# Scores on half the array's rows, the intra product with v streaming, and a DMA transpose for the output

## The chip, the cores and the metric

One core of a Trainium2 chip. It has a matrix engine (TensorE, in the profile PE, its weight loads PEld), three engines that work on vectors (VectorE or DVE, ScalarE or ACT, GpSimd or POOL), a queue processor (SP) and 16 DMA engines. The time is that of one execution on the device in microseconds (us); of several runs the median is given.

## The reference

Two stages. The first is a linear attention with decay, over 4 batches, 8 heads, 768 positions and head size 64; the second an MLP with the Mish function over the 3072 rows that the first gives.

```python
for b in range(nb):                       # blocks along the sequence
    intra = (q_b k_b^T) * Dmask           # lam[h]**(i-j) for i >= j, else 0
    intra = intra @ v_b
    inter = (q_b * lam_pow) @ kv_state
    out[b] = intra + inter
    kv_state = lam_block * kv_state + (k_b * rev_pow)^T @ v_b
x = out as rows of 8 heads x 64           # 3072 x 512
h = x @ w_in                              # 512 -> 2048
out = (h * tanh(softplus(h))) @ w_out     # 2048 -> 512, float32
```

The block size does not matter to the result; the kernel uses blocks of 128 positions.

## The kernel before

The sequence is cut into six **groups** (`NG`) of 128 positions; a group has four **chunks**, one a batch, each of 128 positions and 8 heads. For a group, the MLP works on 4 x 128 = 512 rows: 16 units `mm1_unit` (line 420 for the matmuls, Mish on ScalarE at line 434, result `hsg`) and 16 units `mm2_unit` (line 443; every fourth one ends in a copy by ScalarE and a store to `out`). Every unit is four matmuls with 512 columns.

The order of the program is written out by hand. The loop over groups `n` issues the 32 units of the MLP of group n, and between them the attention **pieces** of group n+1: `room` says after which unit how many pieces follow. Each engine works through its own instructions in that order. In the first place stands `turn` after unit 0, for the first two chunks of the next group.

Group 0 is done ahead in a form of its own (`first_t`, `first_s`, `first_o`): there the scores `pS` of a chunk are computed from `kT[rs]` and `qT[rs]` on 64 rows a head (line 230), the two heads of a pair on the upper and the lower half of the rows, into two tiles. Group 1 turns q and k with TensorE. Groups 2 to 5 are the ones that the change touches. Their q (`qn`) and scaled k (`ktil`, k times a power of lam from `scale_k`, line 259, on POOL except in the last group) are turned by a DMA transpose on SP's queue (`turn`, line 268) into `qraw` and `kraw`, two heads to 128 rows. A chunk is done in two **halves** of four heads, each with three pieces:

- `att_a`: two matmuls `pv` for the state (line 283), into a spare of the MLP's PSUM tiles; VectorE multiplies `qraw` by q's decay `lq` into `qT` (line 318) and copies `kraw` into `kz` (line 322), where each head has its 64 rows and zeros in the other 64; `att_w` brings the state `wst` forward (`raw` on VectorE at 298, `w` on POOL at 299); then `turn` for the chunk after next, or the loads for the next group.
- `att_s`: four score matmuls over all 128 rows (line 358), weights `kz`, moving `qT`; VectorE masks them into `sb` (line 362).
- `att_o`: for each pair of heads one matmul with weights `wst` and moving `qT` (375), and two with weights from `vz` (v with zeros beside it) and moving `sb`, 128 columns (379), so the output comes out turned, features by positions; ScalarE copies it to `xt` (382), the moving operand of `mm1_unit`.

PSUM has eight banks: two each for `ph` and `po` of the MLP, and `pO`, `pS`, `pk`, `pq`, of which the halves of groups 2 to 5 take `pS`/`pk` and `pO`/`pq` in turn. Loads of q, k and v are issued by POOL (lines 69, 77, 80), the stores of `out` by ScalarE.

Of the kernel before, what the change touches and what calls it, by code (L numbers as in the profile page):

```python
# [13 lines left out]
def bc(ap, axis, n):  # L14
    shape = list(ap.shape)
    shape.insert(axis, n)
    return ap.unsqueeze(axis).broadcast_to(shape)
# [3 lines left out]
def kernel(  # L21
# [10 lines left out]
    nc = tc.nc  # L32
# [75 lines left out]
    def load_chunk(i):  # L108
        load_k(i)
        load_q(i)  # L110
        load_v(i)
# [8 lines left out]
    k0 = const.tile([128, H, D], F16, name="k0")  # L120
    q0 = const.tile([128, H, D], F16, name="q0")
    ek = const.tile([128, 1], F32, name="ek")

    load_k(0)
    load_q(0)
# [12 lines left out]
    for s in range(WS):  # L138
        load_wout(s)
    nc.gpsimd.iota(ei, pattern=[[1, C]], base=-MID, channel_multiplier=0,  # L140
                   allow_small_or_imprecise_dtypes=True)
    for i in range(B, 2 * B):
        load_chunk(i)
# [30 lines left out]
    lnp = const.tile([128, JP], F32, name="lnp")  # L174
    lq = const.tile([128, JP, C], F32, name="lq")
    lbc = const.tile([128, JP], F32, name="lbc")

    def decays(t):
        for j in range(JP):
# [11 lines left out]
    def q_decays():  # L191
        nc.vector.tensor_tensor(out=lq, in0=bc(ei, 1, JP), in1=bc(lnp, 2, C), op=ALU.mult)
        nc.scalar.activation(lq, lq, AF.Exp)
        nc.scalar.preload_act_table(AF.Mish)


# [79 lines left out]
    def att_kv(s, spare):  # L276

        n, b, hf = s.n, s.b, s.hf
        i = n * B + b
        pv = ps.tile([128, 2, 128], F32, name="pv", tag=spare, bufs=2)  # L280
        for p in range(2):
            j = 2 * hf + p
            nc.tensor.matmul(  # L283
                pv[:, p, :].rearrange("p (a e) -> p a e", a=2),
                ktil[i][:, 4 * hf + 2 * p : 4 * hf + 2 * p + 2, :].rearrange("p h c -> p (h c)"),
                vz[i % NVB][:, 2 * j : 2 * j + 2, 0:D], start=True, stop=True,
            )
        s.pv = pv
# [17 lines left out]
    def att_a(s):  # L306

        n, b, hf = s.n, s.b, s.hf
        i = n * B + b
        lqh = lq[:, 2 * hf : 2 * hf + 2, :]  # L310
        s.qT = work.tile([128, 2, C], F16, name="qT", tag="qT", bufs=5)
        s.kz = kz[s.seq % NKB]
        kp = [ktil[i][:, 4 * hf + 2 * p : 4 * hf + 2 * p + 2, :].rearrange("p h c -> p (h c)")
              for p in range(2)]
        if n >= NT:
            if n < NG - 1:
                att_kv(s, s.spare)
            nc.vector.tensor_tensor(  # L318
                out=s.qT, in0=qraw[i][:, 2 * hf : 2 * hf + 2, :], in1=lqh, op=ALU.mult)
            for hp in range(2):  # L320
                rs = slice(64 * hp, 64 * hp + 64)
                nc.vector.tensor_copy(s.kz[rs, :, hp, :], kraw[i][rs, 2 * hf : 2 * hf + 2, :])  # L322
            if n < NG - 1:
                att_w(s)
            if hf == 0 and i + 2 < s.loaded:
                turn(i + 2)
            if hf == 1 and i + B < NG * B:
                load_chunk(i + B)
            return
        pk = ps.tile([128, 2, C], F32, name="pk", tag="pk")  # L330
        pq = ps.tile([128, 2, C], F16, name="pq", tag="pq")
        for p in range(2):
            nc.tensor.matmul(pk[:, p, :], kp[p], ident, start=True, stop=True)  # L333
        for p in range(2):
            j = 2 * hf + p
            nc.tensor.matmul(  # L336
                pq[:, p, :], qn[i][:, 2 * j : 2 * j + 2, :].rearrange("p h c -> p (h c)"),
                ident, is_transpose=True, start=(p == 0), stop=(p == 1),
            )
        att_kv(s, s.spare)  # L340
        nc.vector.tensor_tensor(out=s.qT, in0=pq, in1=lqh, op=ALU.mult)
        for hp in range(2):
            rs = slice(64 * hp, 64 * hp + 64)
            nc.scalar.activation(s.kz[rs, :, hp, :], pk[rs], AF.Copy)  # L344
        if hf == 0 and i + 1 < s.loaded:
            scale_k(i + 1)
        elif hf == 0:
            turn(i + 1)
        att_w(s)
        if hf == 1:  # L350
            ahead.pop(0)()

    def att_s(s):

        psS = ps.tile([128, 4, C], F32, name="pS", tag=("pS", "pk")[s.seq % 2 if s.n >= NT else 0])
        for p in range(2):
            for hp in range(2):
                nc.tensor.matmul(  # L358
                    psS[:, 2 * p + hp, :], s.kz[:, p, hp, :], s.qT[:, p, :], start=True, stop=True,
                )  # L360
        s.sb = work.tile([128, 4, C], F16, name="sb", tag="sb", bufs=4)
        nc.vector.tensor_tensor(  # L362
            out=s.sb, in0=psS, in1=bc(maskT, 1, 4), op=ALU.mult)

    def att_o(s):

        n, b, hf = s.n, s.b, s.hf
        i = n * B + b
        if xt[n] is None:
            xt[n] = work.tile([128, JP, GT], F16, name="xt", tag="xt", bufs=2)  # L370
        psO = ps.tile([128, 2, C], F32, name="pO", tag=("pO", "pq")[s.seq % 2 if s.n >= NT else 0])
        vf = vz[i % NVB].rearrange("p h c -> p (h c)")
        for p in range(2):
            j = 2 * hf + p
            nc.tensor.matmul(psO[:, p, :], wst[b][hf][n % 2][:, p, :], s.qT[:, p, :],  # L375
                             start=True, stop=False)
            for hp in range(2):
                o = 4 * D * j + D * hp
                nc.tensor.matmul(psO[:, p, :], vf[:, o : o + 128], s.sb[:, 2 * p + hp, :],  # L379
                                 start=False, stop=(hp == 1))  # L380
        dst = xt[n][:, 2 * hf : 2 * hf + 2, b * C : (b + 1) * C]
        nc.scalar.activation(dst, psO, AF.Copy)  # L382

    seq = [0]

# [127 lines left out]
    for n in range(NG):  # L513
        units = [(mm1_unit, (n, ni)) for ni in range(NKI)]

        two = 2 if n == 0 else 1
        units += [(mm2_unit, (n, b2 + b, part)) for b2 in range(0, B, two) for part in range(WS)
                  for b in range(two)]
        pieces = []
        if n + 1 < NG:  # L520
            pieces = att_pieces(n + 1)
        if n == 0:

            i = max(i for i, (f2, _) in enumerate(pieces) if f2 is att_a)
            pieces[i : i + 3] = pieces[i + 1 : i + 3] + pieces[i : i + 1]

        if n == 0:
            room = dict(zip(range(24, 32), (1, 2, 3, 3, 3, 3, 3, 3)))
        else:
            first = 9 if n == 1 else 6  # L530
            span = len(units) - 4 - first
            room = {first + u: (u + 1) * len(pieces) // span - u * len(pieces) // span
                    for u in range(span)}
        if n == 1:

            for ni in range(3):
                mm1_part(n, ni, 0, GT - C)
                while late and ni < 2:
                    f2, s = late.pop(0)
                    f2(s)  # L540
                    if f2 is att_o:
                        break
        for u, (fn, args) in enumerate(units):
            rest = fn(*args)
            if n > 0 and rest:
                rest()
            if n == 0 and 2 <= u < 2 + nh:
                att_kv(first_halves[u - 2], "po")
                att_w(first_halves[u - 2])
            if n == 0 and u % 2 == 1 and 0 < (u + 1) // 2 < B:  # L550
                scale_k((u + 1) // 2)
            if n == 0 and nh + 2 <= u < nh + 2 + NVB - B:
                nc.vector.memset(vz[u - nh - 2 + B][:, :, D : 2 * D], 0.0)
            if n == 0 and nh + 2 <= u < nh + 2 + NKB:
                nc.vector.memset(kz[u - nh - 2], 0.0)
            if n == 0 and u == 17:
                q_decays()
            if n == 0 and u == 16:
                nc.vector.tensor_scalar(out=maskT, in0=rel, scalar1=0.0, scalar2=None, op0=ALU.is_ge)
            if n == 0 and u == 18:  # L560
                scale_k(B)
            if n > 0 and pieces and u == 0:
                if n > 1:
                    turn((n + 1) * B)
                turn((n + 1) * B + 1)
            for _ in range(room.get(u, 0)):
                f2, s = pieces.pop(0)
                s.spare = "po" if u < NKI - 1 else "ph"
                f2(s)
            if n == 0 and rest:  # L570
                rest()
        if n == 0:
            late = pieces
            while ahead:
                ahead.pop(0)()
# [30 lines left out]
```

## Time and profile before

| | us |
|---|---|
| median of 3 runs (219.08 to 219.74) | 219.31 |
| span of the profiled execution | 218.5 |
| what the median has beside that span | 0.8 |
| TensorE busy in the span | 210.8 (96%) |
| VectorE, ScalarE, POOL busy | 107.5, 104.0, 109.7 |
| first matmul of the MLP of groups 1, 2, 3, 4, 5 | 57.1, 89.2, 122.2, 155.2, 187.3 |

The profile is of one execution; its page gives the span from the first to the last instruction, and no other time of that execution. A line of a group of instructions gives the source line, the engine, the operation, the tiles (written <- read), the shapes and the count; after the bar busy time and the mean duration of one in ns, and after the second bar the engine's idle time ahead of these instructions and what ended it. The duration of a matmul contains the way through the array: consecutive ones overlap, and what one costs is the distance to the start of the next. A line of the chain gives a start, a length, and what ran.

### The profile page before, as it was taken

Reading aid. Unit: us, or ns where it says so; the run is one execution under the profiler, and the core shown is the slowest. Engines: PE = TensorE matmul, PEld = TensorE weight load, DVE = VectorE, ACT = ScalarE, POOL = GpSimd, SP = SyncE. Lnnn points to the kernel's source line nnn. Section 1 sums busy time; section 2 is a strip of 40 time slices with the busy share of each in tenths; the row PEclk is TensorE's granted clock in tenths of the full one; section 3 lists DMA queues with packets and bytes.
Section 4 is the critical chain, followed back from the end, with each engine's and each line's share of the span. In section 5 each row is a group of like instructions: output and inputs, shape, how many; then the busy total and the mean of one; then the engine's idle time right before and its main releaser. Section 6 shows DMA issues by size and latency. Waiting matters only on the chain.

```text
span 218.5 us, 3720 instructions
## 1 busy us (share of the span) xinstructions
PE 210.8 (96%) x1432; PEld 114.4 (52%) x1432; DVE 107.5 (49%) x238; ACT 104.0 (48%) x195; POOL 109.7 (50%) x134
## 2 busy tenths in 40 slices
PE   7799999999999999999999999999999999999993
PEld 2466544577545565455555445556445555444452
DVE  6757661187309995059974049975316532000000
ACT  5355668466665322466332465333466332566120
POOL 7995334889988888239879039775000000000000
PEclk9999999999999999999999999999999999999999
DMA  9999999998999999919999909999921012100112
GB/s 132 146 154 187 205 206 175 156 159 70 179 139 134 120 154 139 205 24 107 105 149 133 182 5 101 116 136 127 195 52 24 0 51 96 48 0 3 48 56 90
DMA packets 101187, 24.62 MB, mean 113 GB/s; under 512 B 93874, under 2 KB 98226, under 8 KB 101170
## 3 DMA queue, kind: packets, MB, share of 16 engines
q0 software_dynamic: 78080, 13.37, 80.7%
q1 hardware_dynamic: 18592, 4.53, 13.7%
q10 hardware_dynamic: 4498, 6.49, 8.7%
q8 instruction: 11, 0.18, 0.3%
q14 instruction: 6, 0.05, 0.1%
HBM read 27.26 MB, written 6.29 MB: 154 GB/s over the span
## 4 chain that ended last, share of the span: by engine, by line
PE 91%; DVE 2%; DMA 2%; ACT 2%; issue 1%; ACTq 0%; DVEq 0%
PE po L443 38%; PE ph L420 37%; PE pS L358 4%; PE pO L379 4%; PE pO L375 2%; PE pv L283 2%; DMA qn<-in_q_dram 2%; PE pO L244 1%; PE busy L162 1%; PE pS L230 1%; DVE sb L234 1%; DVE dm L180 0%; PE pk L333 0%; PE pq L336 0%; DVE pqT L220 0%
## 5 line engine op out<-in xcount | busy, mean ns | idle before, releaser
L443 PE MATMUL po<-wout,hsg 128*128 128x512 f16 (+2 forms) x400 | 92.0, 371 | 0.0
L420 PE MATMUL ph<-xt,win 128*128 128x512 f16 (+2 forms) x404 | 89.8, 369 | 0.4 <-ACT hsg L434 0.2
L434 ACT ACTIVATE hsg<-ph 128x512 f16<-128x512 f32 x96 | 57.0, 597 | 29.9 <-PE ph L420 29.4
L420 PEld LDWEIGHTS <-win 128*128 128x128 f16 x404 | 37.0, 98 | 35.4 <-issue 0.6
L443 PEld LDWEIGHTS <-hsg 128*128 128x128 f16 x400 | 36.2, 98 | 31.7
L299 POOL TENSOR_TENSOR w<-raw,lbm 128x256 f16<-128x256 f32 x32 | 24.3, 760 | 27.6 <-DVE raw L298 27.5
L362 DVE TENSOR_TENSOR sb<-pS,maskT 128x512 f16<-128x512 f32 x40 | 27.4, 684 | 21.4 <-PE pS L358 21.4
L322 DVE COPY kz<-kraw 64x256 f16<-64x256 f16 x64 | 28.9, 452 | 16.3 <-DMA kraw<-ktil 15.3
L455 ACT ACTIVATE osb<-po 128x512 f32<-128x512 f32 (+1 forms) x24 | 14.2, 592 | 41.3 <-PE po L443 41.3
L382 ACT ACTIVATE xt<-pO 128x256 f16<-128x256 f32 x40 | 14.9, 382 | 24.6 <-PE pO L379 22.8
L69 POOL DMA_DIRECT2D kn<-in_k_dram x23 | 21.5, 936 | 4.2 <-DMA win<-in_moe_w_in_dram 1.7
L77 POOL DMA_DIRECT2D qn<-in_q_dram x23 | 20.6, 897 | 5.6 <-DMA wout<-in_moe_w_out_dram 3.3
L80 POOL DMA_DIRECT2D vz<-in_v_dram x24 | 21.7, 904 | 3.3 <-DMA wout<-in_moe_w_out_dram 1.7
L298 DVE TENSOR_TENSOR raw<-pv,w 128x256 f32<-128x256 f32 x32 | 13.5, 422 | 15.9 <-PE pv L283 15.3
L379 PE MATMUL pO<-sb,vz 128*128 128x128 f16 x160 | 17.3, 219 | 0.0
L318 DVE TENSOR_TENSOR qT<-qraw,lq 128x256 f16<-128x256 f16 x32 | 16.8, 524 | 0.0
L259 POOL TENSOR_TENSOR ktil<-kn,lk 128x512 f16<-128x512 f16 x15 | 16.1, 1081 | 0.1
L358 PEld LDWEIGHTS <-kz 128*128 128x128 f16 x160 | 11.9, 98 | 7.9 <-ACT kz L344 0.3
L450 DVE COPY osb<-po 128x128 f32<-128x128 f32 x1 | 0.3, 291 | 32.0 <-PE po L443 32.0
L358 PE MATMUL pS<-qT,kz 128*128 128x128 f16 x160 | 15.6, 219 | 0.1
L375 PE MATMUL pO<-qT,w 128*128 128x128 f16 x80 | 15.3, 219 | 0.1
L379 PEld LDWEIGHTS <-vz 128*128 128x128 f16 x160 | 12.3, 98 | 3.1 <-issue 0.3
(66 smaller groups left out, 118.0 us busy)
## 6 DMA issues: line engine op xcount, KB each, us to landing
out_dram<-osb ACTq DMA_DIRECT2D x23, 256.0 KB, 2.9
vz<-in_v_dram POOLq DMA_DIRECT2D x24, 128.0 KB, 4.9
kn<-in_k_dram POOLq DMA_DIRECT2D x23, 128.0 KB, 4.4
qn<-in_q_dram POOLq DMA_DIRECT2D x23, 128.0 KB, 4.6
wout<-in_moe_w_out_dram POOLq DMA_DIRECT2D x4, 512.0 KB, 16.6
win<-in_moe_w_in_dram POOLq DMA_DIRECT2D x3, 512.0 KB, 10.2
kn<-in_k_dram SPq DMA_DIRECT2D x1, 256.0 KB, 3.1
qn<-in_q_dram ACTq DMA_DIRECT2D x1, 256.0 KB, 3.8
```

Of the source, the lines that this page charges most:

```text
L69: nc.gpsimd.dma_start(out=kn[i], in_=chunk_rows(k, i))
L77: nc.gpsimd.dma_start(out=qn[i], in_=chunk_rows(q, i))
L80: nc.gpsimd.dma_start(out=vz[i % NVB][:, :, 0:D], in_=chunk_rows(v, i))
L299: nc.gpsimd.tensor_tensor(out=w_new, in0=raw, in1=lb, op=ALU.mult)
L322: nc.vector.tensor_copy(s.kz[rs, :, hp, :], kraw[i][rs, 2 * hf : 2 * hf + 2, :])
L358: nc.tensor.matmul(psS[:, 2 * p + hp, :], s.kz[:, p, hp, :], s.qT[:, p, :], start=True, stop=True,)
L362: nc.vector.tensor_tensor(out=s.sb, in0=psS, in1=bc(maskT, 1, 4), op=ALU.mult)
L375: nc.tensor.matmul(psO[:, p, :], wst[b][hf][n % 2][:, p, :], s.qT[:, p, :], start=True, stop=False)
L379: nc.tensor.matmul(psO[:, p, :], vf[:, o : o + 128], s.sb[:, 2 * p + hp, :], start=False, stop=(hp == 1))
L420: nc.tensor.matmul(ph_t[ni][:, lo:hi], win0[min(ni, 2)][:, kc, max(ni - 2, 0) * 128 : max(ni - 2, 0) * 128 + 128] if ni < w else win[ni // ...
L434: nc.scalar.activation(hsg[n][:, ni, :], ph_t.pop(ni), AF.Mish)
L443: nc.tensor.matmul(po[:, lo:hi], hsg[n][:, ki, b * C : (b + 1) * C], wout[part][:, kk, lo:hi], start=(ki == 0), stop=(ki == NKI - 1),)
```

## The change

It is for groups 2 to 5 (`n >= NT`) and leaves groups 0 and 1 as they are. A chunk is no longer cut into halves. Its three pieces are:

- `chunk_a`: four `pv` matmuls into one tile on bank `pq`, the state brought forward in two parts as before, then `turn` for the chunk after next of the group and the loads for the next group. There are no `qT` and no `kz`.
- `chunk_s`: eight score matmuls on 64 rows each, directly from `kraw` and `qraw`, the heads of a pair on different halves of the rows and in different banks (`pS`, `pk`); two masks into `sb`.
- `chunk_o`: the output comes out with positions as rows. For each pair of heads one matmul with weights `qraw` and 128 moving columns of the state, and two with weights `sb` and the 64 columns of a head's v moving. VectorE multiplies the result, while it copies it out of `pO`, by q's decay `lqt` (a number for each position and head) into `xtok`, and a DMA transpose on SP's queue turns it into `xt`.

`lqt` is made once, by a small `iota` on POOL and an exponential on ScalarE. The pieces of a group, twelve in place of 24, stand after units 6 to 23 (9 to 23 for group 2), where the 24 stood after units 6 to 27 (9 to 27).

```diff
+    nc.gpsimd.iota(eq, pattern=[[0, 1]], base=-MID, channel_multiplier=1, ...)
...
+        nc.scalar.activation(lqt, lnb, AF.Exp, scale=eq)
...
-        if n >= NT:
-            if n < NG - 1:
-                att_kv(s, s.spare)
-            nc.vector.tensor_tensor(
-                out=s.qT, in0=qraw[i][:, 2 * hf : 2 * hf + 2, :], in1=lqh, op=ALU.mult)
-            for hp in range(2):
-                rs = slice(64 * hp, 64 * hp + 64)
-                nc.vector.tensor_copy(s.kz[rs, :, hp, :], kraw[i][rs, 2 * hf : 2 * hf + 2, :])
-            if n < NG - 1:
-                att_w(s)
-            if hf == 0 and i + 2 < s.loaded:
-                turn(i + 2)
-            if hf == 1 and i + B < NG * B:
-                load_chunk(i + B)
-            return
...
+    def chunk_a(s):
...
+        if n < NG - 1:
+            pv = ps.tile([128, JP, 128], F32, name="pv", tag="pq")
+            for j in range(JP):
+                nc.tensor.matmul(
+                    pv[:, j, :].rearrange("p (a e) -> p a e", a=2),
+                    ktil[i][:, 2 * j : 2 * j + 2, :].rearrange("p h c -> p (h c)"),
+                    vz[i % NVB][:, 2 * j : 2 * j + 2, 0:D], start=True, stop=True,
+                )
+            for hf in range(2):
+                raw = work.tile([128, 2, 128], F32, name="raw", tag="raw", bufs=3)
+                hs = slice(2 * hf, 2 * hf + 2)
+                nc.vector.tensor_tensor(
+                    out=raw, in0=pv[:, hs, :], in1=wst[b][hf][n % 2], op=ALU.add)
+                nc.gpsimd.tensor_tensor(
+                    out=wst[b][hf][(n + 1) % 2], in0=raw, in1=lbm[:, hs, :], op=ALU.mult)
+        if i + 2 < (n + 1) * B:
+            turn(i + 2)
+        if i + B < NG * B:
+            load_chunk(i + B)
+
+    def chunk_s(s):
...
+        pS = [ps.tile([128, JP, C], F32, name="pS", tag=("pS", "pk")[t]) for t in range(2)]
+        for j in range(JP):
+            for t in range(2):
+                rs = slice(64 * t, 64 * t + 64)
+                nc.tensor.matmul(pS[t][:, j, :], kraw[i][rs, j, :], qraw[i][rs, j, :],
+                                 start=True, stop=True)
+        s.sb = []
+        for t in range(2):
+            s.sb.append(work.tile([128, JP, C], F16, name="sb", tag="sb", bufs=4))
+            nc.vector.tensor_tensor(out=s.sb[t], in0=pS[t], in1=bc(maskT, 1, JP), op=ALU.mult)
+
+    def chunk_o(s):
...
+        psO = ps.tile([128, H, D], F32, name="pO", tag="pO")
+        for j in range(JP):
+            nc.tensor.matmul(
+                psO[:, 2 * j : 2 * j + 2, :].rearrange("p h e -> p (h e)"), qraw[i][:, j, :],
+                wst[b][j // 2][n % 2][:, j % 2, :], start=True, stop=False)
+            for t in range(2):
+                nc.tensor.matmul(psO[:, 2 * j + t, :], s.sb[t][:, j, :],
+                                 vz[i % NVB][:, 2 * j + t, 0:D], start=False, stop=(t == 1))
+        xtok = work.tile([128, H, D], F16, name="xtok", tag="xtok", bufs=2)
+        nc.vector.tensor_tensor(out=xtok, in0=psO, in1=bc(lqt, 2, D), op=ALU.mult)
+        nc.sync.dma_start_transpose(
+            out=xt[n][:, :, b * C : (b + 1) * C], in_=xtok.rearrange("p h e -> p (h e)"))
+
+    def chunk_pieces(n):
...
+        for t in range(B + 1):
+            if t < B:
+                out_ += [(chunk_a, chunks[t]), (chunk_s, chunks[t])]
+            if t >= 1:
+                out_.append((chunk_o, chunks[t - 1]))
+        return out_
...
-            pieces = att_pieces(n + 1)
+            pieces = att_pieces(n + 1) if n + 1 < NT else chunk_pieces(n + 1)
...
-            first = 9 if n == 1 else 6
-            span = len(units) - 4 - first
+            first = 8 if n == 1 else 5
+            span = len(units) - 8 - first
```

More of the change, by code (lines that the diff above doesn't have):

```diff
@@ L122 @@
     ek = const.tile([128, 1], F32, name="ek")
+    eq = const.tile([128, 1], F32, name="eq")
     load_k(0)
@@ L140 @@
     nc.gpsimd.iota(ei, pattern=[[1, C]], base=-MID, channel_multiplier=0,
+                   allow_small_or_imprecise_dtypes=True)
+    nc.gpsimd.iota(eq, pattern=[[0, 1]], base=-MID, channel_multiplier=1,
                    allow_small_or_imprecise_dtypes=True)
@@ L176 @@
     lbc = const.tile([128, JP], F32, name="lbc")
+    lqt = const.tile([128, H], F32, name="lqt")
     def decays(t):
@@ L353, in att_s @@
     def att_s(s):
-        psS = ps.tile([128, 4, C], F32, name="pS", tag=("pS", "pk")[s.seq % 2 if s.n >= NT else 0])
+        psS = ps.tile([128, 4, C], F32, name="pS", tag="pS")
         for p in range(2):
@@ L370, in att_o @@
             xt[n] = work.tile([128, JP, GT], F16, name="xt", tag="xt", bufs=2)
-        psO = ps.tile([128, 2, C], F32, name="pO", tag=("pO", "pq")[s.seq % 2 if s.n >= NT else 0])
+        psO = ps.tile([128, 2, C], F32, name="pO", tag="pO")
         vf = vz[i % NVB].rearrange("p h c -> p (h c)")
@@ L382, in att_o @@
         nc.scalar.activation(dst, psO, AF.Copy)
+    class Chunk:
+        pass
+    def chunk_a(s):
+        n, b = s.n, s.b
+        i = n * B + b
+        if n < NG - 1:
[17 more added lines that the diff above has]
+            load_chunk(i + B)
@@ new lines, in chunk_s @@
+    def chunk_s(s):
+        i = s.n * B + s.b
+        pS = [ps.tile([128, JP, C], F32, name="pS", tag=("pS", "pk")[t]) for t in range(2)]
[8 more added lines that the diff above has]
+            nc.vector.tensor_tensor(out=s.sb[t], in0=pS[t], in1=bc(maskT, 1, JP), op=ALU.mult)
@@ new lines, in chunk_o @@
+    def chunk_o(s):
+        n, b = s.n, s.b
+        i = n * B + b
+        if xt[n] is None:
+            xt[n] = work.tile([128, JP, GT], F16, name="xt", tag="xt", bufs=2)
+        psO = ps.tile([128, H, D], F32, name="pO", tag="pO")
[10 more added lines that the diff above has]
+            out=xt[n][:, :, b * C : (b + 1) * C], in_=xtok.rearrange("p h e -> p (h e)"))
@@ L384 @@
+    def chunk_pieces(n):
+        chunks = []
+        for b in range(B):
+            s = Chunk()
+            s.n, s.b = n, b
+            chunks.append(s)
+        out_ = []
+        for t in range(B + 1):
[4 more added lines that the diff above has]
+        return out_
     seq = [0]
```

## The prediction

> **What bounds the kernel now.** I read the first two parts of the page, then the waits, the chain that ended last, and TensorE in windows cut at the group borders which that chain shows.
>
> ```profile
> span 218.5 us, 3720 instructions
> PE 210.8 (96%) x1432; PEld 114.4 (52%) x1432; DVE 107.5 (49%) x238; ACT 104.0 (48%) x195; POOL 109.7 (50%) x134
> PEclk9999999999999999999999999999999999999999
> ...
> PE ph L420 <- ACT hsg L434: 0.2, 1, 0.2
> ```
>
> TensorE is busy for 96% of the span, and it never waits long for a result: the one wait of its matmuls inside the groups is 0.2 us. The chain names the borders and the windows add up what lies between them (columns: length, then busy time and instructions of each engine, then granted clock).
>
> ```profile
> 89.19 6.04 PE ph L420 x28
> 97.18 0.22 PE pS L358 x4
> 118.72 3.45 PE po L443 x16
> 122.18 6.04 PE ph L420 x28
> ...
> 57.08:89.19 32.11, 31.87 (x229) 17.81 (x228) 20.05 (x40) 14.36 (x28) 28.46 (x33) 1.00 1.76 141
> 89.19:122.18 32.99, 32.99 (x226) 17.89 (x224) 20.64 (x40) 14.68 (x28) 21.08 (x24) 1.00 1.19 119
> 122.18:155.16 32.98, 32.98 (x225) 17.89 (x224) 20.92 (x42) 14.68 (x28) 18.82 (x22) 1.00 1.04 115
> 155.16:187.26 32.10, 32.10 (x210) 16.99 (x208) 12.05 (x33) 14.68 (x28) 0.00 (x0) 1.00 0.21 56
> ```
>
> Those four windows are the four passes of the group loop that carry attention groups 2 to 5, the work that is changed. TensorE fills the last three to the hundredth. A pass has 128 matmuls of 512 columns at 6.04/28 = 0.2157 us, 27.61 us; in the second window the other 5.38 us are 96 attention matmuls of 128 columns, 0.056 each. The last window has 16 `pv` matmuls fewer and is 0.89 shorter: 0.0556 each, which I use. So in these passes time is the number of columns streamed, and whatever leaves TensorE's stream leaves the span, as long as no wait appears.
>
> **TensorE, part by part.** Per chunk (four a pass, 16 in all) the kernel now has 4 `pv`, 8 score and 4 + 8 output matmuls, 24 x 0.0556 = 1.33 us. `pv` stays at four.
>
> *The intra product.* Eight matmuls of 128 columns become eight of 64. No matmul of 64 columns is in the trace. The two known sizes give (215.7 - 55.6)/384 = 0.417 ns a column and 2.2 ns fixed: 28.9 ns for 64. The ends are 26.7 (nothing fixed) and 55.6 (the weights, which still have 128 columns, or the issue set the pace). Two rows speak for the low end, a weight load and the densest burst:
>
> ```profile
> 15.07 0.11 PEld L244 LDWEIGHTS <-vz 128*128 128x128 f16 x2
> 14.74 0.40 PE L230 MATMUL pS<-pqT,pkT 64*128 64x128 f16 x8 [0.30 <-DVE pqT L220]
> 15.07 0.34 PE L244 MATMUL pO<-sb,vz 128*128 128x128 f16 x3
> 16.84 0.39 PE L244 MATMUL pO<-sb,vz 128*128 128x128 f16 x4
> 17.07 0.38 PE L162 MATMUL busy<-kzero 128*128 128x512 f16 x1
> 17.38 0.40 PE L230 MATMUL pS<-pqT,pkT 64*128 64x128 f16 x8
> 17.92 0.32 PE L420 MATMUL ph<-xt,win 128*128 128x384 f16 x1
> ...
> L230 PE MATMUL pS<-pqT,pkT 64*128 64x128 f16 x32 | 2.0, 260 | 1.4 <-ACT pkT L218 0.8 <-DVE pqT L220 0.6
> L358 PEld LDWEIGHTS <-kz 128*128 128x128 f16 x160 | 11.9, 98 | 7.9 <-ACT kz L344 0.3 <-issue 0.2
> ```
>
> Two full weight loads of 98 ns fit in 0.11 us, so a second can start some 10 to 15 ns after the first; and eight 64-row matmuls with eight loads of their own start within 0.40 - 0.22 = 0.18 us, 26 ns apiece. Neither loads nor issue need 55 ns. I take 28.9: 8 x (55.6 - 28.9) = 0.214 us a chunk, 3.42 us in all.
>
> *The scores.* They become eight matmuls on 64 rows in two halves of the array, exactly the form of L230 in group 0, so the price is in the trace. The pairs run side by side, but not for free at the edges. After the 512-column matmul at 17.07 the next should start at 17.07 + 0.216 = 17.29; the 64-row burst starts at 17.38, 0.094 late. The burst at 14.74 is followed by a full-height matmul at 15.07, 0.33 after its first start, where four pairs at 0.0556 are 0.22. So a burst occupies 0.094 + 0.33 = 0.424 us against 8 x 0.0556 = 0.445: 0.02 gained a chunk, 0.33 us in all. The ends: 0.22 without any edge (3.5 us gained), and one more edge of 0.1 (1.3 us lost). The value taken is the row's own, of the same shape behind the same neighbour.
>
> [...]
>
> Sum on TensorE: 1.33 becomes 0.222 + 0.424 + 0.222 + 8 x 0.0289 = 1.10; 16 x 0.235 = 3.75 us less.
>
> **The other engines.**
>
> ```profile
> L322 DVE COPY kz<-kraw 64x256 f16<-64x256 f16 x64 | 28.9, 452 | 16.3 <-DMA kraw<-ktil 15.3
> L362 DVE TENSOR_TENSOR sb<-pS,maskT 128x512 f16<-128x512 f32 x40 | 27.4, 684 | 21.4 <-PE pS L358 21.4
> L318 DVE TENSOR_TENSOR qT<-qraw,lq 128x256 f16<-128x256 f16 x32 | 16.8, 524 | 0.0
> L298 DVE TENSOR_TENSOR raw<-pv,w 128x256 f32<-128x256 f32 x32 | 13.5, 422 | 15.9 <-PE pv L283 15.3
> L299 POOL TENSOR_TENSOR w<-raw,lbm 128x256 f16<-128x256 f32 x32 | 24.3, 760 | 27.6 <-DVE raw L298 27.5
> L382 ACT ACTIVATE xt<-pO 128x256 f16<-128x256 f32 x40 | 14.9, 382 | 24.6 <-PE pO L379 22.8
> L268 SPq DMA_TRANSPOSE qraw<-qn x16: 1188/1212/2046, 51.7 to 158.6; - x16
> DMA to landing us min/median/max: 2.4/3.7/6.3
> ...
> 9.85 0.28 ACT lk L488
> POOL qn L77 <- DMA wout<-in_moe_w_out_dram: 3.3, 2, 1.7
> ```
>
> VectorE loses the `kz` copies and the `qT` products (45.7 us) and gains 16 `xtok` products of the size of `sb`, 0.68 us each; ScalarE loses 32 `xt` copies of 0.38. None of it was on the path, so it is worth nothing by itself; what covers it is the other engines' idle half. The new `iota` stands on POOL in a stretch where POOL waits for weights anyway (3.3 us, last row), the new exponential is one of the size of `lk`, 0.28 us of ScalarE beside the second matmul of group 0: nothing. POOL's `w` products, scalings and loads keep their number, but come in bunches of four a pass, sooner.
>
> *The new waits.* (a) `pO` has one buffer, and the last two output pieces stand one unit apart. The second needs the first's `xtok`: 0.17 us until the last matmul has drained, 0.68, two hand-overs of 0.03: 0.91 us, against a unit of 0.86 and the 0.03 of the last matmul. About 0.06 a pass, 0.25 in all (0 to 0.5). (b) TensorE now reads `kraw` itself, where VectorE used to be late for it without harm (15.3 us of waits in four places). In the later passes eleven units of 0.86 us lie between the piece that turns the last chunk and its scores, and POOL has some 5.5 us to do in between (three loads, two `w`, a scaling), so some 5 us are left for a landing. In the pass from 57.08 it is close: two transposes there start at 64.86 and 73.18, and land 3 to 5 us later:
>
> ```profile
> 64.86 1.19 SPq L268 DMA_TRANSPOSE kraw<-ktil  x1
> 73.18 1.19 SPq L268 DMA_TRANSPOSE kraw<-ktil  x1
> 72.08 1.07 POOL L259 TENSOR_TENSOR ktil<-kn,lk 128x512 f16<-128x512 f16 x1
> ...
> 64.84 0.11 PE pv L283 x2
> ...
> L69 POOL DMA_DIRECT2D kn<-in_k_dram x23 | 21.5, 936 | 4.2 <-DMA win<-in_moe_w_in_dram 1.7
> ```
>
> The first piece stays at 64.84; twelve units of 0.863 and 3.1 us of attention later, at 78.3, the chunk turned by the second is scored, and its transpose lands at 76 to 79: 0.3 us taken, 0 to 1.5. (c) The output goes through SP. Sixteen more transposes of 1.2 us bring SP to 12 a pass, 14 of 32 us. SP takes them in order, behind `kraw` of the last chunk, which waits for POOL; that one is long gone by then. Behind the last `xtok` stand the turns of the next group, needed some 8 us into the next pass. What counts is the last transpose: the next group's first matmul needs all four chunks. Its cover is eight units of the second matmul, 32 x 0.2157 = 6.90 us. Its chain is 0.2 + 0.68, up to 0.7 behind its predecessor on SP, and the landing: 4.6 to 5.3 us at the median of 3.7, 7.2 to 7.9 at the longest. I take 0.25 us over three passes; the fourth has no loads beside it. Ends: 0 and 3.
>
> Sum: -3.75 + 0.25 + 0.3 + 0.25 = -2.95 us. The profiled span goes from 218.5 to 215.6; the median of the runs, 219.31, has 0.8 around that span, and goes to 216.4.
>
> **The rivals.**
> 1. *The output's transpose lands late (slower).* Loads run beside it, and the passes show DMA shares above 1. If each of the first three passes has a landing of 7.5 us instead of 4, TensorE idles 1.5 to 2 us at each border: 3 x 1.8 - 3.2 gives 221.5. It turns the sign from about 7 us a landing on. Against it: no landing of a transpose in the trace is over 6.3.
> 2. *The 64-column matmuls cost 55.6 ns.* Only the 0.33 of the scores is left, less 0.7 of waits: 219.7, no change. The weight-load and burst rows speak against it. [...]
> [...]
> 4. *`kraw` is late for the scores* in the pass from 57.08 and now and then after: 2 us more, 218.4.
>
> **How the numbers follow.** The forecast has 0.58, rival 1 0.15, rival 2 0.11, rival 3 0.05, rival 4 0.11. This kernel's runs tell a change from none from about 0.3%, 0.66 us, on. The forecast, 3 and 4 are faster (0.74); 2 is within (0.11); 1 is slower (0.15). The forecast's own range is 215.3 (nothing waited for, 26.7 ns) to 217.6 (the waits at 0.5, 1.3 and 0.3). The range to hold 8 in 10 reaches down to 214.6, for edges partly hidden, and up to 220.0, which leaves out rival 3 and most of rival 1.
>
> **What would show it.** Right: output matmuls 29 ns apart in the pieces of `sb` and `vz`; a burst of scores 0.42 us from the matmul before to the one after; windows of a pass 0.9 us shorter; no row in which TensorE waits for `xt`. Wrong: `ph` waiting for the transpose at the borders (rival 1), 64-column matmuls 55 ns apart (2), `pS` waiting for `kraw` (4), or POOL's bunched work putting off the turns beyond what I counted.

## The result and the profile after

Over 20 runs each the changed kernel takes 217.99 us (median; 216.82 to 220.39) and the kernel before 219.03 (218.53 to 220.61). The ratio is 0.9934, with a 95% interval from 0.9913 to 0.9955: faster by 0.4 to 0.9%, some 1.4 us. (Ratios, here and below, compare undisturbed runs alone, the medians all of them; in e3, where six of the twelve runs and the profiled one were disturbed, the two differ most.) The profiled execution has a span of 217.1 us against 218.5, and 1.8 us around it. Runs of the kernel before have 1.8 us around their span too (219.09 and 217.3, for one), so the 0.8 between the median and the span profiled before isn't what lies around one execution: that execution was one of the longer ones. The forecast takes the same saving off both and isn't hurt by it.

The head of the page of the changed kernel, then two groups of TensorE's instructions by line, the new intra product and the scores:

```profile
span 217.1 us, 3664 instructions
PE 208.3 (96%) x1432; PEld 106.2 (49%) x1432; DVE 76.6 (35%) x158; ACT 93.2 (43%) x164; POOL 108.0 (50%) x135
...
q0 software_dynamic: 78080, 13.37, 85.2%
q1 hardware_dynamic: 27296, 6.63, 20.9%
```

```profile
L427 PE MATMUL pO<-vz,sb 128*128 128x64 f16 x128 | 9.0, 193 | 0.0
...
L408 PE MATMUL pS<-qraw,kraw 64*128 64x128 f16 x128 | 6.4, 219 | 0.0
```

TensorE has 2.5 us less work (210.8 to 208.3), VectorE 30.9 and ScalarE 10.8. The queue of SP's transposes (q1) carries 27,296 packets, whose times add up to 20.9% of the engines' time; those of POOL's loads (q0) add up to 85.2%. (Over a short stretch such a share can pass 100%: from 116 to 118 us, further below, q0's is 242.4%.)

To see where the time went, I cut both traces at the same five places: the first 512-column matmul `ph` of groups 1 to 5. (For the first pass this lies after the shorter matmuls at its border, so these marks differ a little from the prediction's.) Kernel before, then changed kernel; the columns are those of the prediction's windows:

```profile
58.63:89.03 30.40, 30.40 (x213) 16.71 (x213) 19.38 (x38) 13.33 (x26) 26.91 (x31) 1.00 1.81 142
89.03:122.01 32.98, 32.98 (x225) 17.89 (x224) 20.64 (x40) 14.68 (x28) 21.08 (x24) 1.00 1.20 119
122.01:155.00 32.99, 32.99 (x225) 17.89 (x224) 20.92 (x42) 14.68 (x28) 18.82 (x22) 1.00 1.03 115
155.00:187.09 32.09, 32.09 (x209) 16.99 (x208) 12.05 (x33) 14.68 (x28) 0.00 (x0) 1.00 0.23 56
```

```profile
58.87:90.50 31.63, 29.82 (x213) 14.55 (x212) 10.92 (x20) 11.08 (x19) 26.48 (x31) 1.00 1.89 149
90.50:122.67 32.17, 32.17 (x225) 15.82 (x226) 10.92 (x20) 11.34 (x19) 20.25 (x24) 1.00 1.44 134
122.67:154.84 32.17, 32.17 (x226) 15.80 (x224) 12.73 (x23) 11.94 (x20) 18.20 (x22) 1.00 1.33 132
154.84:186.14 31.30, 31.30 (x210) 14.85 (x209) 8.52 (x13) 11.94 (x20) 0.00 (x0) 1.00 0.38 85
```

Three passes are 0.8 us shorter each (0.81, 0.82, 0.79), with TensorE full to the hundredth. The first pass is 1.23 us *longer*, and TensorE stands still in it for 1.81 us. Together the four passes are 1.19 us shorter; the MLP of the last group behind them is unchanged (27.6 us in both).

The chain that ended last (start, length, what ran) shows both places where TensorE stands in the first pass, and the waits name them:

```profile
74.69 6.25 DMA xt<-xtok
...
81.03 0.70 DVE xtok L430
...
81.78 0.22 PE pO L423
...
82.39 6.91 PE po L507 x32
89.30 1.20 issue
90.50 6.20 PE ph L484 x28
```

```profile
DVE xtok L430 <- DMA xt<-xtok: 1.7, 2, 0.9
...
PE ph L484 <- issue: 1.2, 1, 1.2
...
PE pO L423 <- DVE xtok L430: 0.6, 1, 0.6
```

First place: `xtok` has two buffers. The third chunk's product must wait until the first chunk's transpose has read its buffer, and that transpose, for which the chain has 74.69, ends 6.25 us later. VectorE therefore makes the third `xtok` at 81.03; `pO` has one buffer, so the fourth chunk's output matmuls, due at 81.00, wait until 81.78. The first `xtok` and SP's queue, by time:

```profile
L430 DVE TENSOR_TENSOR xtok<-pO,lqt x1: 692/692/692, 71.3 to 71.3; 128x512 f16<-128x512 f32 x1
...
73.41 1.19 SPq L273 DMA_TRANSPOSE kraw<-ktil  x1
74.69 9.90 SPq L431 DMA_TRANSPOSE xt<-xtok  x4
```

That first `xtok` is there at 72.0, but its transpose is issued 2.7 us later: SP takes its transposes in the program's order, and this one stands behind the fourth chunk's `kraw`, which goes out at 73.41, as soon as POOL has made that chunk's scaled k. POOL begins that only at 72.32, behind three loads (68.26 to 70.95) and two state products; without the loads (e4, below) it begins at 69.20. So the buffer is held for 2.7 us of waiting on SP and 6.25 us of transfer.

Second place: the last two transposes land at 88.91 and 90.41, and the next group's first matmul starts at 90.50 instead of 89.14 (one matmul after the last `po`): 1.36 us. The profile calls the idle time "issue"; that it is the landing of `xt` is what the experiments have to show. Landings of the transposes of `xtok` in four stretches: the whole run, 75 to 90, 90 to 122 and 155 to 190 us (the last has no loads beside it):

```profile
DMA to landing us min/median/max: 2.4/6.0/7.2
DMA to landing us min/median/max: 6.2/7.1/7.2
DMA to landing us min/median/max: 5.8/6.3/7.0
DMA to landing us min/median/max: 2.4/2.4/3.5
```

SP's queue around the border of the second and third pass, then what the DMA queues handled from 116 to 118 us and from 118 to 122.5 us (packets, MB, share):

```profile
115.28 2.62 SPq L431 DMA_TRANSPOSE xt<-xtok  x2
118.00 1.21 SPq L273 DMA_TRANSPOSE qraw<-qn  x1
```

```profile
q0 software_dynamic: 2445, 0.31, 242.4%
q1 hardware_dynamic: 4, 0.00, 0.4%
...
q1 hardware_dynamic: 1958, 0.48, 102.6%
q0 software_dynamic: 497, 0.06, 21.2%
```

Two transposes of `xt` are issued from 115.28 on. While POOL's loads run through the engines, SP's queue gets four packets in 2 us against 2445; the transposes move only when the loads thin out. They land at 122.25 and 122.47, just in time: the next group starts at 122.67. At the border of the third and fourth pass the last one lands at 154.57, and the next group starts at 154.84.

### The profile page after: what moved, and what is told of

The parts are those of the page before. It is cut to its first block, busy times and chain, and to the rows that moved or that the text cites. A ratio compares the mean times of both kernels' runs of the same rounds, so it can differ in the third digit from the quotient of the medians.

```text
span 217.1 us, 3664 instructions
## 1 busy us (share of the span) xinstructions
PE 208.3 (96%) x1432; PEld 106.2 (49%) x1432; DVE 76.6 (35%) x158; ACT 93.2 (43%) x164; POOL 108.0 (50%) x135
## 3 DMA queue, kind: packets, MB, share of 16 engines
q0 software_dynamic: 78080, 13.37, 85.2%
q1 hardware_dynamic: 27296, 6.63, 20.9%
## 4 chain that ended last, share of the span: by engine, by line
PE 88%; DMA 5%; DVE 3%; issue 2%; ACT 2%; ACTq 0%; DVEq 0%
PE ph L484 38%; PE po L507 36%; DMA xt<-xtok 3%; PE pS L408 2%; DMA qn<-in_q_dram 2%; PE pO L423 2%; PE pO L427 1%; PE pO L249 1%; PE pv L384 1%; PE busy L165 1%; PE pS L235 1%; PE pS L348 1%; PE pv L288 1%; PE pO L369 1%; DVE sb L239 1%
## 5 line engine op out<-in xcount | busy, mean ns | idle before, releaser
L413 DVE TENSOR_TENSOR sb<-pS,maskT 128x512 f16<-128x512 f32 x32 | 20.6, 686 | 31.1 <-PE pS L408 31.1
L394 POOL TENSOR_TENSOR w<-raw,lbm 128x256 f16<-128x256 f32 x24 | 17.2, 752 | 24.1 <-DVE raw L392 24.1
L430 DVE TENSOR_TENSOR xtok<-pO,lqt 128x512 f16<-128x512 f32 x16 | 11.1, 692 | 8.1 <-PE pO L427 5.4
L165 PE MATMUL busy<-kzero 128*128 128x512 f16 x18 | 8.5, 573 | 1.2 <-DVE kzero L150 1.2
L423 PE MATMUL pO<-w,qraw 128*128 128x128 f16 x64 | 9.0, 220 | 0.6 <-DVE xtok L430 0.6
L427 PEld LDWEIGHTS <-sb 128*128 128x128 f16 x128 | 7.9, 98 | 2.7 <-issue 1.3
L427 PE MATMUL pO<-vz,sb 128*128 128x64 f16 x128 | 9.0, 193 | 0.0
L264 DVE TENSOR_TENSOR ktil<-kn,lk 128x512 f16<-128x512 f16 (+1 forms) x9 | 6.0, 685 | 5.6 <-DMA kn<-in_k_dram 5.6
L334 ACT ACTIVATE kz<-pk 64x256 f16<-64x256 f32 x16 | 6.0, 377 | 4.0 <-PE pk L323 3.4
L423 PEld LDWEIGHTS <-qraw 128*128 128x128 f16 x64 | 6.3, 98 | 2.2 <-DVE xtok L430 0.4
```

The costliest lines, as they stand in the source:

```text
L264: (nc.vector if i <= B or i >= (NG - 1) * B else nc.gpsimd).tensor_tensor(out=t, in0=kn[i], in1=bc(lk, 2, D), op=ALU.mult)
L394: nc.gpsimd.tensor_tensor(out=wst[b][hf][(n + 1) % 2], in0=raw, in1=lbm[:, hs, :], op=ALU.mult)
L413: nc.vector.tensor_tensor(out=s.sb[t], in0=pS[t], in1=bc(maskT, 1, JP), op=ALU.mult)
L423: nc.tensor.matmul(psO[:, 2 * j : 2 * j + 2, :].rearrange("p h e -> p (h e)"), qraw[i][:, j, :], wst[b][j // 2][n % 2][:, j % 2, :], start ...
L427: nc.tensor.matmul(psO[:, 2 * j + t, :], s.sb[t][:, j, :], vz[i % NVB][:, 2 * j + t, 0:D], start=False, stop=(t == 1))
```

## The experiments

The passes of all kernels, cut as above (us). "Sum" is that of the four passes. The execution of each kernel is one; passes without a wait repeat to 0.01 or 0.02 us, but a wait need not repeat. Each ratio is to runs of the kernel before made beside that kernel's runs, with medians of 219.72 (e1 to e4), 219.84 (e5, e6) and 219.53 us (e7, e8).

| kernel | first | second | third | fourth | sum | median of runs | ratio to before, 95% |
|---|---|---|---|---|---|---|---|
| before | 30.40 | 32.98 | 32.99 | 32.09 | 128.46 | 219.03 | |
| after | 31.63 | 32.17 | 32.17 | 31.30 | 127.27 | 217.99 | 0.9934 (0.9913 to 0.9955) |
| e1 four `xtok` | 31.38 | 32.17 | 32.45 | 31.29 | 127.29 | 218.21 | 0.9928 (0.9894 to 0.9962) |
| e2 128 columns | 31.58 | 33.03 | 33.02 | 32.15 | 129.78 | 221.00 | 1.0045 (1.0012 to 1.0077) |
| e3 `kz` again | 32.37 | 32.52 | 33.69 | 31.33 | 129.91 | 220.88 | 0.9990 (0.9950 to 1.0031) |
| e4 no loads | 29.58 | 32.17 | 32.17 | 31.30 | 125.22 | 215.44 | 0.9801 (0.9752 to 0.9849) |
| e5 loads held back | 30.65 | 32.17 | 32.17 | 31.30 | 126.29 | 215.49 | 0.9825 (0.9769 to 0.9881) |
| e6 and pieces apart | 30.64 | 32.09 | 32.09 | 31.20 | 126.02 | 216.72 | 0.9852 (0.9801 to 0.9903) |
| e7 and one `ktil` on VectorE | 29.58 | 32.09 | 32.10 | 31.20 | 124.97 | 216.21 | 0.9846 (0.9806 to 0.9886) |
| e8 e5 with two `xtok` | 30.48 | 32.17 | 32.17 | 31.29 | 126.11 | 216.52 | 0.9881 (0.9837 to 0.9925) |

The theory behind them: TensorE's saving is as predicted, and the first pass gives it back because transposes take 6 to 7 us beside POOL's loads. The rivals were that the `xtok` buffers alone are to blame, and that the saving itself is smaller than it seems.

**e1: four buffers for `xtok`.**

```diff
-        xtok = work.tile([128, H, D], F16, name="xtok", tag="xtok", bufs=2)
+        xtok = work.tile([128, H, D], F16, name="xtok", tag="xtok", bufs=4)
```

> Four buffers for xtok in place of two; nothing else. In the changed kernel the third output piece of the pass from 57.3 finds both buffers still being read by transposes, and TensorE loses 0.77 us there; the last two transposes land 7.1 us after their issue and the MLP of group 2 starts 1.36 us late. Theory (a landing takes its own 7 us from the issue on): the 0.77 goes to 0.08 and, since the last two transposes are issued 0.7 us sooner, the 1.36 falls to about 0.7; 1.4 us less in all, ratio to the kernel before 0.987. Rival (the DMA engines are full and a transpose lands when the loads ahead of it are through): the 0.77 goes, the border waits as much longer, nothing gained, ratio 0.993.

The end of the first pass in the chain of e1, then two of its waits:

```profile
86.44 1.64 issue
```

```profile
PE ph L484 <- issue: 1.6, 1, 1.6
...
PEld L484 <- DMA xt<-xtok: 0.6, 1, 0.6
```

The wait at `pO` is gone, and the last two output pieces run in their places. But the border now waits longer (1.80 us against 1.36), and another 0.28 appears in the third pass. The last transpose is issued 0.9 us sooner after the first mark than in the changed kernel, and lands 0.25 us sooner. The sum is the same to 0.02 us, with 0.25 gained in the first pass and 0.28 lost in the third. So more buffers alone don't bring the time back: of the 0.9 us by which that transpose is issued sooner, 0.25 are left at its landing. The theory that the buffers alone were to blame falls.

**e2: the intra product streams 128 columns again** (the zeros beside v with it), all else as changed.

```diff
-                nc.tensor.matmul(psO[:, 2 * j + t, :], s.sb[t][:, j, :],
-                                 vz[i % NVB][:, 2 * j + t, 0:D], start=False, stop=(t == 1))
+                o = 4 * D * j + D * t
+                nc.tensor.matmul(
+                    psO[:, 2 * j : 2 * j + 2, :].rearrange("p h e -> p (h e)"), s.sb[t][:, j, :],
+                    vz[i % NVB].rearrange("p h c -> p (h c)")[:, o : o + 128],
+                    start=False, stop=(t == 1))
```

> The intra product streams 128 columns again (v with the zeros beside it, both heads of the pair written), output positions by features and everything else as in the changed kernel. Theory (columns streamed set the cost, the weight loads are hidden): 128 matmuls go from 28.9 to 55.6 ns, 3.4 us more, ratio 1.009. Rival (the gain of the change came from elsewhere, weight loads or issue set the pace of the 64-column matmuls): no change, ratio 0.993.

The three later passes are 0.86, 0.85 and 0.85 us longer than after: 32 matmuls at 26.7 ns each, the predicted 55.6 - 28.9. The first pass is 0.05 *shorter*: with TensorE slower there, the wait at `pO` disappears and the border waits 1.16 us, against 1.36 after. The slower TensorE hides part of the late transfer; that is why undoing this part alone costs 2.5 us and not 3.4. The verdict follows: 1.0045, slower than the kernel before. Of the 3.5 us that TensorE saves in all (e7), 3.4 sit in the 64 columns.

**e3: the scores on 128 rows again**, with copies of `kraw` into `kz` and unscaled q.

```diff
+    def spread(i):
+        for hf in range(2):
+            for t in range(2):
+                rs = slice(64 * t, 64 * t + 64)
+                nc.vector.tensor_copy(
+                    kz[2 * (i % 2) + hf][rs, :, t, :], kraw[i][rs, 2 * hf : 2 * hf + 2, :])
...
-                rs = slice(64 * t, 64 * t + 64)
-                nc.tensor.matmul(pS[t][:, j, :], kraw[i][rs, j, :], qraw[i][rs, j, :],
-                                 start=True, stop=True)
+                nc.tensor.matmul(pS[t][:, j, :], kz[2 * (i % 2) + j // 2][:, j % 2, t, :],
+                                 qraw[i][:, j, :], start=True, stop=True)
```

> The scores use all 128 rows again: kraw is copied into kz with zeros beside each head (64 copies on VectorE, as before), the moving operand is qraw, eight matmuls one after the other. Theory (a burst on 64 rows pays 0.21 us at its edges and so costs 0.425 against 0.445): the scores cost 0.02 us more a chunk, 0.3 us in all, edges gone, ratio 0.995, up to 0.998 if the copies are late for a chunk. Rival (pairs side by side are a real gain of 0.2 us a chunk): 3.4 us more, ratio 1.009.

The last pass of e3, then two waits:

```profile
157.84:189.17 31.33, 31.33 (x208) 16.06 (x209) 12.57 (x30) 11.34 (x19) 0.00 (x0) 1.00 0.33 84
```

```profile
DVE kz L381 <- DMA kraw<-ktil: 28.8, 8, 7.7
...
PE pS L418 <- DVE kz L381: 0.8, 2, 0.4
```

In the pass without loads the two forms differ by 0.03 us over four chunks (31.33 against 31.30): eight matmuls on 64 rows in two halves of the array take almost as long as eight on 128 rows. The rival that the pairs save 0.2 us a chunk falls. Passes one to three are 0.35 to 1.5 us longer, in an execution that is one of the longer ones of e3 (221.89 us, the shortest 217.76), so the sizes of its waits are its own: VectorE now waits for `kraw` in front of `kz`, the `sb` and `xtok` products stand behind that wait on VectorE, and the borders wait 1.2, 0.3 and 1.0 us. Of TensorE's own time the scores on 64 rows save next to nothing; what they may bring is that VectorE no longer stands between `kraw` and TensorE, but by how much this one execution doesn't show.

**e4: no loads for groups 3 to 5.**

```diff
     def load_chunk(i):
+        if i >= 3 * B:
+            kn[i], qn[i] = kn[i - B], qn[i - B]
+            return
```

> Leaves out the loads of q, k and v of groups 3 to 5, whose attention takes q and k of group 2 and v as it lies in the buffers; all else as in the changed kernel. Theory (the loads beside them make the output's transposes land late): landings of xt fall from 6 to 7 us to 2.4 to 3.5 in all passes, the wait of 1.36 us at the border and 0.7 of the 0.77 at the third output piece go, ratio 0.984. Rival (the transposes are slow by themselves, or by their own number): landings stay at 6 us and both waits stay, ratio 0.993.

The first pass of e4, then its landings of `xtok`:

```profile
58.41:87.99 29.58, 29.57 (x212) 14.65 (x212) 10.93 (x20) 10.49 (x18) 15.83 (x19) 1.00 1.10 120
```

```profile
DMA to landing us min/median/max: 2.4/3.7/5.0
```

Both waits vanish at once, with two `xtok` buffers in place. The first pass takes 29.58 us, so after's 31.63 hold 2.05 us more: 1.36 at the border, and at `pO` the 0.78 from above less 0.09 that e4 waits there too. Landings go from a median of 6.0 back to 3.7, and the first transpose of the pass is issued at 72.1, 0.6 us after its `xtok` is made. The loads of the group after next, which POOL issues ahead, are the cause; whether by their transfers or by POOL's time for issuing them, this run doesn't tell, since it leaves out both.

**e5: the last loads of a pass held back.** Four `xtok`; the loads of the last two chunks of the group after next are issued behind the last `xtok` of a pass, held there by a copy of one of its columns on POOL. The work is that of the changed kernel.

```diff
-        if i + B < NG * B:
+        if b < B - 2 and i + B < NG * B:
             load_chunk(i + B)
...
+        if b == B - 1 and n < NG - 1:
+            gate = work.tile([128, 1], F16, name="gate", tag="gate", bufs=2)
+            nc.gpsimd.tensor_copy(gate, xtok[:, 0, 0:1])
+            load_chunk(i + B - 1)
+            load_chunk(i + B)
```

> Four buffers for xtok, and the loads for the last two chunks of the group after next stand behind the last output piece of a pass: a copy of one column of the last xtok on POOL holds them back until that xtok is there. Theory (six loads issued in the 7 us before the last two transposes stand ahead of them in the DMA engines): the last two transposes land 3 to 5 us after their issue and the next pass starts on time, so all four passes run at TensorE's sum, 32.1 us with pv and 31.3 without; 3.3 us less than before from the first pass to the last matmul, ratio 0.985. Rival (the sixteen transposes more are too much for SP or the engines whatever the order of the loads): the border waits stay at 1 us or more, or the held-back loads make kraw late for the third chunk of the next pass and TensorE waits for it in pS; ratio 0.99 or above.

The landings of `xtok` in e5, and the wait that is new:

```profile
DMA to landing us min/median/max: 2.4/4.5/6.3
```

```profile
PE pS L408 <- DMA kraw<-ktil: 1.0, 1, 1.0
```

With all the loads done and only their time moved, no border waits any more: `xt` lands after 4.5 us at the median. The first pass still has 1.07 us over 29.58, now at another place: the second chunk's scores wait for `kraw`. This is the prediction's wait (b), which does not appear in the profile of the changed kernel. That `kraw` lands 5.3 us after its issue here and 5.1 in e6. In the changed kernel, e1, e2 and e8, whose code is the same up to there, it lands after 3.6 or 3.7 us, and no matmul waits. So this wait comes and goes between executions, and its cause is open.

**e6: e5, and the third chunk's output piece one unit earlier** in the passes after the first. (In the first, the two units that the edit swaps hold one piece each, and nothing changes.)

```diff
+        if n >= 1 and n + 1 < NG:
+            u2 = [u for u in sorted(room) if room[u]][-2]
+            room[u2], room[u2 - 1] = room[u2 - 1], room[u2]
```

> As the gated kernel, and in the passes after the first the output piece of the third chunk stands one unit sooner, two units ahead of that of the fourth. Theory: the 0.08 us that TensorE waits for pO in each of these three passes goes, 0.25 us in all, ratio 0.984. Rival: the wait moves to the piece that was brought forward, which then stands one unit behind the last scores, and nothing changes.

Passes two to four fall from 32.17, 32.17 and 31.30 to 32.09, 32.09 and 31.20: 0.08 to 0.10 each. That is the wait for the one buffer of `pO`, predicted at 0.06.

**e7: e6, with the scaled k of the second chunk of group 2 made by VectorE.**

```diff
-        (nc.vector if i <= B or i >= (NG - 1) * B else nc.gpsimd).tensor_tensor(
+        (nc.vector if i <= B or i == 2 * B + 1 or i >= (NG - 1) * B else nc.gpsimd).tensor_tensor(
```

> As the spread kernel, and the scaled k of the second chunk of group 2 is made by VectorE instead of by POOL, where it stands behind the issue of seven loads. In the gated kernel's profile TensorE waits 1.1 us for that chunk's kraw in the pass from 57.5 (1.0 in the spread one), in an execution that came to that pass 1.3 us sooner than the changed kernel's. Theory (a quick start is eaten up by that wait): the wait goes, the pass takes 29.7 us between its full-size matmuls in place of 30.65, 1.0 us less where the start is quick, ratio 0.980. Rival (the loads of q in flight hold that transpose, not POOL): kraw lands at the same time, ratio 0.984.

The first pass of e7:

```profile
58.78:88.36 29.58, 29.58 (x212) 14.62 (x212) 11.61 (x21) 10.48 (x18) 23.71 (x30) 1.00 1.83 142
```

The wait for `kraw` is absent and TensorE is full. That the edit removed it is not shown. The `kraw` is issued 2.7 us sooner after the first mark than in e5, but takes 6.2 us to land, so it is there 9.7 us after the mark; in e8, with that chunk's scaled k still made by POOL, it is there after 9.9 us, and nothing waits either. The four passes sum to 124.97 us, 3.49 less than before: nearly the whole saving of the change, with one wait of 0.09 left, at `pO` in the first pass (81.00, due at 80.91). In the runs' times e5, e6 and e7 cannot be told apart (216.21 us here, 215.49 and 216.72 there, each with 2 to 3.5 us between its runs); much of that spread lies ahead of the passes, as the last section shows.

**e8: e5 with two `xtok` buffers.**

```diff
-        xtok = work.tile([128, H, D], F16, name="xtok", tag="xtok", bufs=4)
+        xtok = work.tile([128, H, D], F16, name="xtok", tag="xtok", bufs=2)
```

> The gated kernel with two buffers for xtok again. Theory (the loads of the pass itself hold the first transposes too, so the buffer wait of the first pass has its own cause): 0.5 to 0.8 us more than the gated kernel in the pass from 57, later passes the same, ratio 0.985. Rival (holding back the loads frees the buffers in time): same as the gated kernel.

The wait in its first pass:

```profile
PE pO L423 <- DVE xtok L430: 0.8, 1, 0.8
```

With the loads held back and two buffers the borders stay free, but the 0.90 us over 29.58 sit at `pO` again. The first transpose of the pass still stands behind `kraw` on SP (issued at 73.64, its `xtok` made at 70.9) and lands after 6.4 us. So the two waits end by different means. The border needs the loads moved. `pO` needs a free buffer in time: by more buffers (e1, e7), or by transposes that start and land sooner (e4).

## Why the prediction was right and where it was not

The sign was right; the predicted 216.4 us is 1.6 below the median. In the profile the span fell by 1.4 us where 2.95 was predicted. The first mark lies 0.24 us later and the passes are 1.19 shorter; the rest, some 0.4, is behind the last matmul.

*The intra product: right.* 64 columns with full weights go 28 to 29 ns apart. The first and the last line of an output piece with its neighbour, by time:

```profile
103.04 0.22 PE L423 MATMUL pO<-w,qraw 128*128 128x128 f16 x1
103.09 0.22 PE L427 MATMUL pO<-vz,sb 128*128 128x64 f16 x2
...
103.49 0.60 PE L484 MATMUL ph<-xt,win 128*128 128x512 f16 x2
```

The piece takes 0.45 us (103.04 to 103.49), where 0.222 + 8 x 0.0289 = 0.453 was predicted. Rival 2 (55.6 ns) is out, by these rows and by e2.

*The scores on 64 rows: right.* The burst between two matmuls of the MLP:

```profile
97.62 1.03 PE L484 MATMUL ph<-xt,win 128*128 128x512 f16 x4
98.58 0.40 PE L408 MATMUL pS<-qraw,kraw 64*128 64x128 f16 x8
98.91 0.61 PE L484 MATMUL ph<-xt,win 128*128 128x512 f16 x2
```

Four matmuls from 97.62 end their turn at 97.62 + 4 x 0.2157 = 98.48; the burst starts at 98.58 and the next matmul at 98.91. That is 0.10 at the edge and 0.33 for the burst, the 0.424 of the row in group 0. Rival 3 (no edges) is out.

*The sum on TensorE: right,* 3.58 us (e7's 3.49 and its wait of 0.09) against 3.75. The missing 0.17 is 0.01 a chunk, about what can be read from rows given to 0.01 us.

*Wait (a), `pO`: its size in the first pass failed.* Predicted 0.25 in all; after has 0.78 in the first pass, and 0.08, 0.08 and 0.10 (e6) in the others: 1.04. The 0.06 a pass for the single `pO` was about right. What the step left out is that `xtok` has two buffers, and that a transpose holds each from the time it is made until it has landed: 2.7 us behind `kraw` on SP's queue and 6.25 us of transfer. The prediction looked at that queue for the last transpose alone, where `kraw` is indeed long gone; for the first one it isn't. (Its last sign of being wrong, POOL's bunched work putting off the turns, names this.)

*Wait (b), `kraw`: the cover held,* 0 where 0.3 was taken. The cover is thin: e5 shows the wait at 1.0 us and e6 at 0.8, with code that is the same up to there.

*Wait (c), the last output transpose: this is the step that failed.* The cover of 6.90 us was right (the chain shows 32 matmuls in 6.91). The landing was taken at the median before, 3.7 us, with 0.25 us over three passes as the price. The landings are 6.0 at the median and up to 7.2, and the first border alone cost 1.36. Rival 1 named this mechanism and put its turning point at 7 us; its argument against, that no landing before was over 6.3, took the longest landing of a different pattern as a bound. The change puts four more transposes into each pass, in three of the four behind POOL's bunched loads. What kept the sign is that it happened at one border and not at three, and that is luck: at the other two the last landing was ahead of the next group's start by 0.20 and 0.27 us, and in e1 the third pass lost 0.28.

So -3.58 + 1.04 + 0 + 1.36 = -1.18, against the measured -1.19. The terms come from the same windows, so that they add up is bookkeeping; only the 0.78 and the 1.36 were read by themselves, from the rows. The median's part is as uncertain as the start of the runs (below).

## What to carry to other kernels

On TensorE, full to the hundredth in three of the four passes, a saving computed per instruction arrived to within 0.01 us a chunk (3.58 us of 3.75); what has to be predicted is the waits, and a transfer's duration must be priced for the traffic at its new place, not by the median of its old one (6.0 us against 3.7 here). When a result moves from an engine's copy to a DMA, follow the buffer as well as the consumer: the first `xtok` stayed occupied while its transfer waited behind another on SP's queue (2.7 us) and until it had landed (6.25 us). And when a transfer is late beside prefetches, try to move the prefetches before adding buffers: here loads held back, with the buffers and two small moves (e7), gave the passes another 2.3 us, of which 1.07 is a wait that may have been absent by chance; buffers alone (e1) gave nothing.

## What the runs showed that was not expected

*The queue.* From 116 to 118 us SP's queue handled 4 packets and POOL's 2445, with two transposes already issued. From 118 to 122.5 us it was 1958 against 497. Whether the engines hold the transposes back or their packets are made late isn't told by the trace; e4 shows only that without the loads a landing is at most 5.0 us.

*The start.* Executions of one kernel spread by 2 us and more. Much of that lies ahead of the first pass, as far as the kept traces show: in the changed kernel, e1 to e3 and e5 to e8, whose code is the same up to there, the first mark lies between 56.70 (e1) and 59.26 us (e3). Four preparing matmuls and the four behind them, of the changed kernel and then of e1, whose code is the same up to there:

```profile
13.33 0.63 PE L217 MATMUL pk<-ident,kn 128*128 128x128 f16 x4
13.76 0.63 PE L217 MATMUL pq<-ident,qn 128*128 128x128 f16 x4
```

```profile
11.54 0.39 PE L217 MATMUL pk<-ident,kn 128*128 128x128 f16 x4
11.76 0.39 PE L217 MATMUL pq<-ident,qn 128*128 128x128 f16 x4
```

Four matmuls take 0.43 us in the one and 0.22 in the other: 13 us into the span of the first, TensorE still takes twice as long for them. At 14.18 us a matmul of 512 columns takes 0.63 us there; in e1 one takes 0.38 at 8.33 us already, so the quicker pace is reached at least 5.8 us apart in the two. The granted clock reads 1.00 there in both profiles, but the trace's records of the clock begin only at 15.1 us in the first, with full speed; in e4 the clock is 0.984 over the whole span. That a lower clock is behind the slower matmuls is an estimate from these numbers; what sets the time at which they get quicker, the traces don't tell. In the changed kernel and in e1 the first pass then starts at 58.87 and at 56.70. Cutting the traces from the first pass on takes this spread out of the comparison.
